# First 512 tokens from four batches instead of four chunks of one: a recurrence with a feed-forward layer on one core

## The chip, the cores and the metric

The kernel runs on one core of a Trainium2 chip. The time is device microseconds (us), the median of several executions. The kernel before took 190.63 us (three runs, 190.18 to 190.70) when the prediction was made and 190.66 beside the changed kernel (four runs, one of them in the slow state with 193.85). The ratios below use runs in the fast state alone.

## The reference

Gated linear attention (four batches, eight heads, 768 tokens, head size 48), then a feed-forward layer with a squared relu on the 3072 tokens.

```python
for t in range(S):                                   # q, k, v, alpha: [4, 8, 768, 48]
    state = alpha[:, :, t, :, None] * state + np.einsum('bhd,bhe->bhde', k[:, :, t], v[:, :, t])
    y[:, :, t] = np.einsum('bhd,bhde->bhe', q[:, :, t], state)
x = y.transpose(0, 2, 1, 3).reshape(3072, 384)
out = np.maximum(x @ w_in, 0.0) ** 2 @ w_out         # w_in 384 x 2048, w_out 2048 x 384
```

## The kernel before

Tokens are worked on in 24 chunks of 128. For a chunk, ScalarE takes the logarithm of alpha, TensorE sums it up along the tokens, ScalarE makes the exponentials A and 1/A, VectorE multiplies q and k with them, TensorE transposes both and forms scores, VectorE masks these, and TensorE multiplies with v and reads and updates the state. The result is transposed (xT) and goes through the feed-forward layer. A scheduler in the kernel, which works with fixed durations, fixes the order of instructions on each engine. What it costs when the next one in that order has to wait is seen below (ScalarE lost 13.7 us so).

The first four chunks are done together, with wide first loads, and are the four chunks of one batch, so their state updates follow one another:

```python
slot_srcs = {n: a[0, :, 0:4 * P, :].rearrange("h (p j) d -> p h (j d)", j=4) for n, a in srcs}
...
def load_slots(nm, lo, hi):                  # two of these for alpha and two for q
    nc.sync.dma_start(out=slot[nm][:, lo:hi].rearrange("p h j d -> p h (j d)"),
                      in_=slot_srcs[nm][:, lo:hi])
```

Later chunks have four loads each. SyncE issues alpha, q and k as fp32 (five buffers each); GpSimd issues v, which its queue casts to bf16 on the way (six buffers). SyncE also issues the output, one write per tile of 128 rows:

```python
LB = 5; LBV = 6
...
(nc.gpsimd if pool or nm == "vt" else nc.sync).dma_start(out=d[nm], in_=src[b, c])
...
nc.sync.dma_start(out=out_r[GT[g] + tt], in_=box["ob"])
...
hold_x(C[6], C[5], "at")      # SyncE's loads of chunk 6 and later start when chunk 5's alpha is there
```

## Time and profile before

| | before |
|---|---|
| time, span | 190.63 us, 189.4 us |
| TensorE, VectorE, ScalarE, GpSimd busy | 95%, 70%, 67%, 22% of the span |
| first feed-forward matmul | 22.50 us |
| TensorE in every stretch from 60 us to 172 us | full |

The prediction below shows the busy tenths, the chain and the start. What it does not show, and what turned out to matter, is the loads of later chunks. These are lines of the timeline of SyncE (start, us of issuing, queue, line, transfer): the alpha loads of chunks 10 to 13.

```profile
54.70 0.59 SPq L339 DMA_DIRECT2D at<-in_alpha_dram  x1
...
57.38 1.63 SPq L339 DMA_DIRECT2D at<-in_alpha_dram  x1
...
62.40 1.70 SPq L339 DMA_DIRECT2D at<-in_alpha_dram  x1
...
66.56 1.07 SPq L339 DMA_DIRECT2D at<-in_alpha_dram  x1
```

Alpha is a chunk's first load and first need. Here one follows the other about every 4 us, and in the stretch from 20 to 100 us ScalarE's logarithm is never listed as waiting for one. TensorE in two stretches (length, then busy time and count of PE, PEld, DVE, ACT, POOL, then TensorE's clock, DMA share, GB/s):

```profile
60.00:74.00 14.00, 14.00 (x168) 10.94 (x166) 11.59 (x26) 10.71 (x27) 3.73 (x6) 1.00 1.34 173
74.00:88.00 14.00, 14.00 (x159) 10.73 (x157) 11.70 (x31) 10.25 (x32) 3.90 (x8) 1.00 1.30 187
```

### The profile page before, as it was taken

The page shows a single profiled execution, that of the slowest core. Times are in us where ns is not written, and L with a number is a line of the kernel's source. Part 1 is how long each engine was busy: PE and PEld are TensorE (multiplying, and loading weights), DVE is VectorE, ACT ScalarE, POOL GpSimd, SP SyncE. Part 2 cuts the span into 40 slices and gives each one's busy share as a digit, 9 for nine tenths or more (in the row PEclk, how much of TensorE's full clock was granted, in tenths as well). Part 3 has the DMA queues.
Part 4 walks back from the last instruction along what each step waited for, and adds up shares of the span by engine and source line. Part 5 has one row for each costly group of instructions (what it writes and reads, how often), then busy time and mean ns, then how long its engine had stood idle before and what let it go on. Part 6 is the DMA issues. An engine that isn't in the chain of part 4 may idle for free.

```text
span 189.4 us, 5215 instructions
## 1 busy us (share of the span) xinstructions
PE 180.2 (95%) x1999; PEld 137.1 (72%) x1999; DVE 132.3 (70%) x335; ACT 126.7 (67%) x346; POOL 42.2 (22%) x78
## 2 busy tenths in 40 slices
PE   7864999999999999999999999999999999999993
PEld 2553778866878887777777787787787787777773
DVE  3167946754899795897886886886886886944411
ACT  3763459926778886678588588488588586565630
POOL 8967335023122233222021031041000000000000
PEclk9998589999999999999999999999999999999999
DMA  5999999899999999999959739739011011011112
GB/s 177 238 165 203 204 223 211 125 183 147 183 191 185 206 180 173 201 153 188 218 130 142 166 84 124 170 87 126 0 45 43 3 42 45 6 37 45 42 42 83
DMA packets 94280, 24.71 MB, mean 130 GB/s; under 512 B 85216, under 2 KB 93920, under 8 KB 94256
## 3 DMA queue, kind: packets, MB, share of 16 engines
q1 hardware_dynamic: 64992, 17.45, 44.8%
q0 software_dynamic: 29120, 6.88, 37.5%
q8 instruction: 15, 0.25, 0.6%
q14 instruction: 9, 0.07, 0.1%
q10 hardware_dynamic: 144, 0.05, 0.1%
HBM read 25.17 MB, written 4.72 MB: 158 GB/s over the span
## 4 chain that ended last, share of the span: by engine, by line
PE 87%; DMA 5%; SPq 3%; ACT 1%; DVE 1%; issue 1%; ACTq 0%; DVEq 0%
PE bank L226 78%; PE bank L229 7%; DMA kt<-in_k_dram 5%; PE st L226 2%; SPq L339 2%; SPq L319 1%; ACT r L668 1%; DVE st L578 1%; DVE sm L533 1%; ACT sb L583 0%; ACT xn L220 0%; DVE ob L736 0%; ACT ob L736 0%; ACT L_s L442 0%; DVE kI_s L474 0%
## 5 line engine op out<-in xcount | busy, mean ns | idle before, releaser
L668 ACT ACTIVATE r<-bank 128x256 bf16<-128x256 f32 (+1 forms) x160 | 64.7, 429 | 29.6 <-PE bank L226 28.2
L226 PE MATMUL bank<-xT_big,w_in_b 128*128 128x256 bf16 (+1 forms) x624 | 80.0, 266 | 0.1
L226 PE MATMUL bank<-w_out_b,gT 128*128 128x384 bf16 (+1 forms) x400 | 74.7, 320 | 0.0
L226 PEld LDWEIGHTS <-w_in_b 128*128 128x128 bf16 x624 | 53.8, 98 | 9.7 <-issue 0.5
L675 DVE TENSOR_TENSOR gT<-r 128x256 bf16<-128x256 bf16 (+1 forms) x160 | 47.6, 315 | 16.0 <-ACT r L668 14.4
L226 PEld LDWEIGHTS <-gT 128*128 128x128 bf16 x400 | 37.9, 98 | 15.8
L533 DVE TENSOR_TENSOR sm<-bank,utri_b 128x512 bf16<-128x512 f32 x40 | 25.3, 683 | 2.6 <-PE bank L226 2.5
L339 POOL DMA_DIRECT2D vt<-in_v_dram x24 | 21.3, 888 | 7.9 <-POOL vt L338 6.1
L338 POOL CAST vt<-kt 128x1 bf16<-128x1 f32 x18 | 4.7, 263 | 64.6 <-PE bank L226 41.8
L471 DVE TENSOR_TENSOR qA_s<-qt,A 128x384 bf16<-128x384 f32 x20 | 11.1, 556 | 9.5 <-ACT A L458 8.6
L218 DVE COPY qkT<-bank 128x1024 bf16<-128x1024 bf16 x20 | 13.8, 688 | 4.9 <-PE bank L229 4.9
L474 DVE TENSOR_TENSOR kI_s<-kt,Ainv 128x384 bf16<-128x384 f32 x24 | 13.3, 556 | 3.1 <-DMA kt<-in_k_dram 2.6
L709 ACT COPY ob<-bank 128x384 f32<-128x384 f32 x21 | 10.1, 480 | 8.1 <-PE bank L226 8.1
L226 PEld LDWEIGHTS <-qkT 64*128 64x128 bf16 (+1 forms) x260 | 10.4, 97 | 5.9 <-issue 2.5
L220 ACT CAST xn<-bank 128x384 bf16<-128x384 f32 x23 | 10.9, 480 | 4.2 <-PE bank L226 3.8
L583 ACT CAST sb<-st 128x384 bf16<-128x384 f32 x20 | 9.6, 478 | 5.7 <-DVE st L578 5.7
L458 ACT ACTIVATE A<-bank 128x384 bf16<-128x384 f32 x20 | 9.9, 496 | 2.4 <-PE bank L226 2.4
L229 PE MATMUL bank<-ident_bf,kI_s 128*128 128x128 bf16 x96 | 9.5, 223 | 2.1 <-DVE kI_s L474 2.1
L578 DVE TENSOR_TENSOR st<-st,ae_s 128x384 f32<-128x384 f32 x20 | 11.1, 556 | 0.0
L442 ACT ACTIVATE L_s<-at 128x384 bf16<-128x384 f32 x20 | 10.4, 521 | 0.0
L462 ACT ACTIVATE Ainv<-bank 128x384 bf16<-128x384 f32 x20 | 10.2, 510 | 0.0
L229 PE MATMUL bank<-ident_bf,qA_s 128*128 128x128 bf16 x96 | 9.3, 219 | 0.8 <-DVE qA_s L407 0.7
(78 smaller groups left out, 162.1 us busy)
## 6 DMA issues: line engine op xcount, KB each, us to landing
out_dram<-ob SPq DMA_DIRECT2D x23, 192.0 KB, 2.7
kt<-in_k_dram SPq DMA_DIRECT2D x21, 192.0 KB, 5.3
at<-in_alpha_dram SPq DMA_DIRECT2D x18, 192.0 KB, 4.8
qt<-in_q_dram SPq DMA_DIRECT2D x18, 192.0 KB, 4.7
vt<-in_v_dram POOLq DMA_DIRECT2D x24, 96.0 KB, 5.6
w_in_b<-in_moe_w_in_dram POOLq DMA_DIRECT2D x4, 384.0 KB, 11.0
w_out_b<-in_moe_w_out_dram POOLq DMA_DIRECT2D x4, 384.0 KB, 12.3
slot_at<-in_alpha_dram SPq DMA_DIRECT2D x2, 384.0 KB, 3.6
```

The costliest lines, as they stand in the source:

```text
L218: pin(nc.vector.tensor_copy(out, in_))
L220: pin(nc.scalar.copy(out, in_))
L226: pin(nc.tensor.matmul(*a, **kw))
L229: pin(nc.tensor.transpose(*a))
L339: pin((nc.gpsimd if pool or nm == "vt" else nc.sync).dma_start(out=d[nm], in_=src[b, c]))
L442: pin(nc.scalar.activation(L[:, :, 0:D], d["at"], AF.Ln))
L471: pin(nc.vector.tensor_mul(qA[:, :, 0:D], d["qt"], d["A"]))
L474: pin((nc.vector if mk.eng == "DVE" else nc.gpsimd).tensor_mul(kI[:, :, 0:D], d["kt"], d["Ai"]))
L533: pin(nc.vector.tensor_mul(d["sm"][:, hh], d["sc"][hh], (utri_p if first else utri_b).to_broadcast([P, NP, P])))
L578: pin(nc.vector.tensor_mul(st4, st4, bcast(ae, D)))
L668: pin(nc.scalar.activation(box["r"], box["ph"], AF.Relu))
L675: pin(nc.vector.tensor_mul(gT[g][:, f0:f0 + nf, 0:n], box["r"], box["r"]))
```

## The change

The intent is to rid the start of the chain of four state updates: the first chunk of each batch needs no state, so the four first chunks can be done side by side. Partition 4g+b holds the four consecutive tokens 4g to 4g+3 of batch b. Several things come with it: each of alpha, q and k is loaded by four DMAs over 32 partitions, v comes as fp32, through SyncE's queue for all chunks but 4 and 5 (GpSimd loads these two), and is cast by GpSimd (for two of the first four chunks by ScalarE), there are four load buffers instead of five (and four for v instead of six), and the output of the first four tiles, whose rows are out of order, is written in four pieces each.

```diff
-    slot_srcs = {n: a[0, :, 0:4 * P, :].rearrange("h (p j) d -> p h (j d)", j=4) for n, a in srcs}
+    rows = {n: a[:, :, 0:P, :].rearrange("b h (g j) d -> b g h (j d)", j=NJ) for n, a in srcs}
+    v_rows = v[:, :, 0:P, :].rearrange("b h (g j) d -> j g (b h) d", j=NJ)
+    SEQ = [(b, 0) for b in range(B)] + [(b, c) for b in range(B) for c in range(1, NCH)]
-    LB = 5
-    LBV = 6
+    LB = 4
-    opool = ctx.enter_context(tc.tile_pool(name="opool", bufs=8))
+    opool = ctx.enter_context(tc.tile_pool(name="opool", bufs=5))
...
+            pin(q.dma_start(out=slot[nm][b::B], in_=rows[nm][b]))          # b = 0..3; 32 partitions each
...
-                pin((nc.gpsimd if pool or nm == "vt" else nc.sync).dma_start(out=d[nm], in_=src[b, c]))
+                pin((nc.gpsimd if pool else nc.sync).dma_start(out=C[s][nm], in_=srcs[nm][c, :, b * H:(b + 1) * H]))
...
+        def e_vb():
+            d["vb"] = work.tile([P, H, D], BF16, name="vb", bufs=4)
+            pin(nc.gpsimd.tensor_copy(d["vb"], d["vt"]))
...
-            pin(nc.sync.dma_start(out=out_r[GT[g] + tt], in_=box["ob"]))
+            if SEQ[GT[g] + tt][1] == 0:
+                for j in range(NJ):
+                    pin(nc.sync.dma_start(out=out_tile(GT[g] + tt)[j], in_=ob[j * PQ:(j + 1) * PQ]))
+            else:
+                pin(nc.sync.dma_start(out=out_tile(GT[g] + tt), in_=ob))
```

## The prediction

> **What bounds the kernel now.** I read the page's busy tenths first, then the chain that ended last in order of time, then the first 30 us of the timeline.
>
> ```profile
> PE   7864999999999999999999999999999999999993
> DVE  3167946754899795897886886886886886944411
> PEclk9998589999999999999999999999999999999999
> DMA  5999999899999999999959739739011011011112
> ```
>
> Each digit is 4.73 us. TensorE is full from the fifth slice on; only the first four have holes, and slice 5 runs at half clock. The DMA engines are busy for half the run, but TensorE does not wait for them after the start. The chain says where the start ends:
>
> ```profile
> 6.33 9.01 DMA kt<-in_k_dram
> 15.50 0.34 issue
> 15.84 0.56 DVE st L578
> 16.40 0.96 DVE sm L533 x2
> ...
> 22.50 15.27 PE bank L226 x139
> ...
> 167.36 18.95 PE bank L226 x152
> 186.33 0.25 ACT ob L736
> ```
>
> Until 22.50 the path is a load (the third k tile, 9.01 us from issue to landing), then the state chain of four sequential chunks; from 22.50, the first feed-forward matmul, it is TensorE to 186.3. A table of stretches confirms it (us, busy and counts of PE, PEld, DVE, ACT, POOL, then clock, DMA, GB/s):
>
> ```profile
> 16.00:22.50 6.50, 5.49 (x63) 3.88 (x63) 6.23 (x12) 3.81 (x9) 3.08 (x5) 0.64 1.25 206
> 22.50:40.00 17.50, 17.50 (x168) 13.99 (x169) 11.20 (x25) 12.13 (x25) 6.28 (x9) 0.94 1.18 187
> ```
>
> So the time is: start (22.5) + TensorE work left at that moment + tail (3.0, to 189.4), and the device time is 1.2 above the span (190.63 against 189.4). After 22.5 come 163.8 us. Steady state has a period of 13.94 us for two tiles (the same piece of the chain, 4.83 us of feed-forward matmuls, begins at 100.28 and again at 114.22), 6.97 per tile, of which streaming 48x128 plus 16x384 columns at the full rate is about 5.2 and attention about 1.75. 24x5.2 + 20x1.75 + 2.8 left from the first four chunks = 162.6, plus 1.1 for half clock until 24.7: 163.7. The sum closes, so nothing else is hidden there. The change can gain only (a) by an earlier start, (b) by less TensorE work after it.
>
> **What the Trainium skill says.** "TensorE: Matmul & The Clock Gate", Part 1, has the clock halved after an idle window and restored after about 3.4 us of sustained activity. The trace agrees: granted clock 0.53 in the stretch 20 to 25 us, 1.00 from 25 on. The same must be paid again after any new start. "DMA: Bandwidth & Descriptors", section Issuing engines are not separate DMA queues, says that loads from several issuers share the same 16 engines and only issue time is saved; here the k tile that took 9.01 us was issued by SyncE while GpSimd had v and k tiles under way, which fits. "SBUF — State Buffer", section Who interferes with whom, says that a VectorE instruction with two SBUF inputs contends with a GpSimd instruction that reads SBUF. No trace of before shows it (GpSimd's only casts are 128x1); the change makes it possible. The same page, section Door 1: The DMA port swizzle, charges strided reads that leave a 16-byte line. The trace fits: the three matmuls that transpose xn against a strided identity take 0.81 us even at full clock, 390 ns each against 219 for a plain transpose.
>
> **The change part by part.**
>
> Removed: the four chunks of one batch as the first 512 tokens, with their state chain (4 rounds of matmul, 0.56 VectorE, 0.48 ScalarE) between 15.8 and 22.3 us. In its place stand the first chunks of four batches, which need no state. Their state updates, and the transposes back of k that they need, move behind the start of the feed-forward part.
>
> TensorE work, from durations back to back at full clock (transpose 0.056, state matmul 0.043, score 0.04, 48-column 0.032, 96-column 0.06, 384-column 0.16, 4-column 0.03 us). Before, first four chunks: 16 matmuls of 32 rows, about 0.6; 16 cumulative of 384 columns, 2.6; 32 transposes 1.8; 16 sums 0.5; scores 1.3; sm x v 1.0; state reads 0.7; state 0.7; the strided xn transposes 12x0.27 = 3.2: 12.4. After: the 32-row ones are gone; cumulative 2.7 in 28 pieces; transposes 1.8; sums 0.5; scores 1.3; sm x v 1.0; plain xn transposes 12x0.056 = 0.7: 8.0. Later 16 transposes of k 0.9, state 0.7, state reads 0.7: 10.3 in all. Work saved 2.1, but it is saved in the start. Left over once the feed-forward part runs (read off the timeline after 22.5): before 2.8, of which two strided xn transposes are 1.6; after 2.3 plus the end of chunks three and four, 0.6: 2.9. Part (b) is nil. **The gain is the start alone.**
>
> Start after, step by step. Alpha: before, its halves (393 KB each) landed at 4.13 and 5.30, so 336 GB/s; now four pieces, two of them behind ScalarE's 1.28 us table load: about 5.2. ScalarE is then the busiest engine: 4 logs at a pitch of 0.43 (7.0), 8 exponentials at 0.42 and two small ones at 0.2 (10.8), six copies at 0.48 (13.7). K lands after 2x786 KB more at 336 GB/s, 4.7 us: 9.9; VectorE then makes four k products and the last q product at a pitch of 0.5 (12.4), its transpose 0.4, its copy is ScalarE's last, done about 13.8. Scores 0.4 (14.2); the masks' second halves, 4x0.36 on VectorE (15.8); product with v 0.4 twice (16.6); xn 0.5, transpose 0.4, xT 0.5 and a few hand-overs: **first feed-forward matmul at 18.2** (17.2 to 20). Before: 22.5. Gain 4.3.
>
> The weights are now held until k has landed: issued from 10 us, so w_in's first quarter (before: issued 8.85, landed 8.7 later behind v and k tiles) should land at 15 to 17 with only v in its way. Just in time. v is 786 KB in 192-byte pieces, about 4 us after k: 14; its casts are then not the last thing.
>
> Against that: half clock. VectorE and ScalarE pace TensorE from 10 to 18 us, so it will be cold again; before, 2.2 us at half clock fell after 22.5 (loss 1.1). Starting at 18.2, I expect about 4 us cold: loss 2.0, so 0.9 more. And 0.7 for new holes (below). Sum: -4.3 + 0.9 + 0.7 = -2.7; 190.6 - 2.7 = **187.9 us**.
>
> Beside other work: v is loaded as fp32 by SyncE (24.7 MB become about 27, but no casting queue), and 22 casts of 128x384 go to GpSimd, which is 22% busy. From a 128x128 select at 0.30 and a 128x512 iota at 0.57 I estimate 0.5 each, 11 us in all, off the path. Output rows in four pieces for the first four tiles: issue time on SyncE, off the path.
>
> **The rivals.**
>
> *A late weight takes the place of the wait.* If k lands at 12 rather than 10 (small pieces on 32 partitions being slower than 336 GB/s), everything after shifts by 2, and w_in, held behind it, lands at 18 to 19 or later. The start would be 20.5 to 22 and the time 189.5 to 191. For it: k is the end of before's path. Against it: 768-byte pieces instead of 192, and no GpSimd traffic beside them.
>
> *VectorE becomes the bound.* In program order it gets 15 output copies instead of 2 (13x0.56 = 7.3 us more, ScalarE 6.3 less) and meets the casts' reads. In the fullest stretch it was busy 17.36 of 20 us; 13 copies over 110 us add about 1.3 per 20. 93% plus lock waits could open holes in TensorE: 1 to 4 us, 189 to 191.5. Against it: its waits were mostly for ScalarE's relu, which gets lighter. I charge 0.7 of it, with late chunk 4 and 5 loads and the run of first-layer matmuls on which ScalarE's relu leaves little slack.
>
> *The start is better than worked out.* If TensorE stays warm and ScalarE's two alpha loads issue at once, the start is 17 and no cold loss: 185.5 to 186.5.
>
> **Range and chances.** The centre is 187.9 (1.4% less); the 2% line is at 186.8, 1.1 below it. The start's uncertainty is 1.2, the clock's 1, the holes' 1; together about 1.8. Range 185.9 to 190.2. Faster by over 2%: 0.28; within: 0.62; slower by over 2% (194.4, only if VectorE or the loads starve TensorE for over 6 us): 0.10.
>
> **What would show it.** First feed-forward matmul near 18 us; clock 0.5 for some 4 us about it; the chain before it through ScalarE and VectorE, with no state line; TensorE without holes afterwards; xn transposes near 220 ns; casts near 0.5 us. I am wrong if that first matmul waits for w_in, if TensorE shows waits for VectorE in 60 to 160, or if the start is at 18 and the time still the same.

## The result, and the profile after

The changed kernel took 199.02 us (median of four runs, 197.50 to 200.06) against 190.66: slower, ratio 1.044 with a 95% interval of 1.035 to 1.053. Ratios here are the mean time of one kernel's fast runs over the mean of the other's fast runs of the same rounds, so they are not quite the ratio of the medians. The result is correct. The profiled run took 197.5 us with a span of 195.8. It is the fastest of the four: the other spans are 196.2 to 198.2, and no trace shows where these runs lost more.

The busy tenths of the changed kernel (a digit is 4.9 us):

```profile
PE   7776999999997947999999999999999999999993
DVE  5199479686975916797788798897897888855531
PEclk9996699999999996999999999999999999999999
DMA  5999999989997979999589379659610011011112
```

TensorE now has a hole where the line of before had only nines: slices 13 to 16 read 7, 9, 4, 7, at 59 to 78 us. VectorE dips there too, to 5 and 1, so it is not VectorE's load that holds TensorE up. The rest of the line is full. The stretches of before, again:

```profile
60.00:74.00 14.00, 9.59 (x105) 7.33 (x103) 8.22 (x21) 9.02 (x21) 1.19 (x2) 1.00 0.86 160
74.00:88.00 14.00, 13.38 (x125) 10.14 (x126) 10.88 (x26) 7.95 (x25) 1.01 (x2) 0.88 1.29 204
```

TensorE is busy for 9.59 of 14 us, then loses more to a clock of 0.88 and another 0.6 us of idling. The chain that ended last, asked for this stretch alone (start, us, what):

```profile
55.69 0.42 SPq L772
...
56.21 4.09 DMA at<-in_alpha_dram
...
60.38 0.52 ACT L_s L500
60.91 0.97 ACT r L718 x2
...
65.22 0.43 SPq L772
...
66.78 5.63 DMA at<-in_alpha_dram
...
72.86 0.58 ACT r L718
```

The path leaves TensorE. It goes through SyncE's queue issuing output pieces (L772), then an alpha load of 4 to 5.6 us, then ScalarE's logarithm of it (L500), then the relu of the feed-forward layer (L718), which stands behind that logarithm in ScalarE's order. The longest hole shows the same from both sides, in the timelines of ScalarE and TensorE:

```profile
72.43 0.52 ACT L500 ACTIVATE L_s<-at 128x384 bf16<-128x384 f32 x1 [4.11 <-DMA at<-in_alpha_dram]
...
74.62 0.50 PE L210 MATMUL bank<-ident_bf,xn 128*128 128x128 bf16 x3 [3.75 <-ACT xn L201]
```

ScalarE waits 4.11 us for the alpha of chunk 12, and TensorE 3.75 us for the copy xn, which also stands behind that logarithm (it runs at 74.07). In the list of waits for 20 to 100 us there is a line that before has not (total us, count, longest):

```profile
ACT L_s L500 <- DMA at<-in_alpha_dram: 13.7, 7, 4.1
```

SyncE's timeline tells why alpha is late:

```profile
53.88 2.23 SPq L772 DMA_DIRECT2D out_dram<-ob  x4
56.21 0.40 SPq L431 DMA_DIRECT2D at<-in_alpha_dram  x1
56.65 0.58 SPq L431 DMA_DIRECT2D qt<-in_q_dram  x1
57.33 3.21 SPq L772 DMA_DIRECT2D out_dram<-ob  x4
60.59 0.42 SPq L431 DMA_DIRECT2D kt<-in_k_dram  x1
61.11 0.53 SPq L431 DMA_DIRECT2D vt<-in_v_dram  x1
61.73 0.75 SPq L431 DMA_DIRECT2D at<-in_alpha_dram  x1
...
66.78 0.92 SPq L431 DMA_DIRECT2D at<-in_alpha_dram  x1
...
73.69 0.65 SPq L431 DMA_DIRECT2D at<-in_alpha_dram  x1
```

SyncE issues almost without a gap. Alpha of chunks 10 to 13 goes out at 56.2, 61.7, 66.8 and 73.7, where before it went out at 54.7, 57.4, 62.4 and 66.6: some 5.8 us apart instead of 4. The four groups of four pieces (two are shown; the others took 2.30 and 3.59 us) hold SyncE for 11.3 us in all between 53.9 and 72.2, and the v loads for another part. The pieces were not late themselves: their tiles had been copied out by 49.7, 52.0, 55.9 and 60.2, and their first pieces went out at 53.9, 57.3, 63.3 and 68.6.

The start, from the timelines of ScalarE, VectorE and TensorE:

```profile
6.72 1.76 ACT L341 ACTIVATE L_f<-slot_at 128x384 bf16<-128x384 f32 x4 [4.64 <-DMA slot_at<-in_alpha_dram]
...
11.75 1.96 DVE L361 TENSOR_TENSOR qk_f<-slot_kt,Ainv 128x384 bf16<-128x384 f32 x4 [0.48 <-ACT ae L395]
...
16.91 0.92 ACT L201 CAST vb<-v 128x384 bf16<-128x384 f32 x2 [1.46 <-DMA v<-in_v_dram]
...
20.44 0.80 PE L207 MATMUL bank<-xT_big,w_in_b 128*128 128x256 bf16 x3 [0.25 <-ACT xT_big L201]
```

Alpha is there at 6.7, k at about 11.7, v at 16.9, and the first feed-forward matmul runs at 20.44, 2.06 us earlier than before.

**Where the time went.** I added up, for each trace, what TensorE's matmuls cost at full rate (columns over 2400 us plus 2.5 ns, at least 32 ns: 0.163 us for 384 columns, 0.109 for 256 and 0.056 for 128, which are the distances between the starts of such matmuls back to back in both traces; for 48 columns the traces have 0.025, so the small ones are charged too much; warm-up matmuls count nothing). It is an estimate, made the same way for all kernels. The sum is the work; the time minus the work done so far is what TensorE has lost by then.

| | work in all | lost by 30 us | by 60 | by 81 | at the end |
|---|---|---|---|---|---|
| before | 175.4 | 13.6 | 13.7 | 13.4 | 14.0 |
| after | 173.7 | 14.0 | 14.7 | 21.4 | 22.1 |

The work fell by 1.7 us, the loss by 30 us rose by 0.4: the new start is worth 1.3 us. Between 30 and 81 us the changed kernel loses 7.4 us and the other gains 0.2 (the cost at full rate is slightly overestimated), so the new holes cost 7.6. The sum is 6.3, and the spans differ by 6.4.

### The profile page after: what moved, and what is told of

It is laid out like the page before. It is cut to its first block, busy times and chain, and to the rows that moved or that the text cites. A ratio compares the mean times of both kernels' runs of the same rounds, so it can differ in the third digit from the quotient of the medians.

```text
span 195.8 us, 5297 instructions
## 1 busy us (share of the span) xinstructions
PE 181.7 (93%) x2011; PEld 138.9 (71%) x2011; DVE 143.2 (73%) x357; ACT 124.4 (64%) x340; POOL 30.4 (16%) x56
## 4 chain that ended last, share of the span: by engine, by line
PE 68%; DMA 18%; SPq 5%; ACT 3%; issue 2%; POOL 2%; DVE 1%; POOLq 0%; ACTq 0%
PE bank L207 61%; DMA at<-in_alpha_dram 11%; PE bank L210 6%; DMA w_in_b<-in_moe_w_in_dram 5%; SPq L319 3%; DMA slot_kt<-in_k_dram 2%; SPq L772 2%; PE st L207 2%; ACT r L718 1%; POOL w_in_b L269 1%; ACT L_s L500 1%; SPq L431 1%; DVE kI_s L527 0%; ACT A L511 0%; ACT Ainv L515 0%
## 5 line engine op out<-in xcount | busy, mean ns | idle before, releaser
L718 ACT ACTIVATE r<-bank 128x256 bf16<-128x256 f32 (+1 forms) x160 | 64.6, 429 | 28.3 <-PE bank L207 27.2
L207 PE MATMUL bank<-w_out_b,gT 128*128 128x384 bf16 (+1 forms) x400 | 75.7, 322 | 0.0
L725 DVE TENSOR_TENSOR gT<-r 128x256 bf16<-128x256 bf16 (+1 forms) x160 | 49.2, 329 | 19.3 <-ACT r L718 17.5
L493 POOL CAST vb<-vt 128x384 bf16<-128x384 f32 x20 | 12.2, 609 | 99.9 <-PE bank L207 65.3
L500 ACT ACTIVATE L_s<-at 128x384 bf16<-128x384 f32 x20 | 10.4, 521 | 13.7 <-DMA at<-in_alpha_dram 13.7
L199 DVE COPY qkT<-bank 128x1024 bf16<-128x1024 bf16 x20 | 13.7, 686 | 3.5 <-PE bank L210 3.4
L524 DVE TENSOR_TENSOR qA_s<-qt,A 128x384 bf16<-128x384 f32 x20 | 11.4, 569 | 3.4 <-ACT A L511 2.7
L762 DVE COPY ob<-bank 128x384 f32<-128x384 f32 x15 | 8.4, 557 | 7.5 <-PE bank L207 7.4
L210 PE MATMUL bank<-ident_bf,xn 128*128 128x128 bf16 x72 | 8.4, 234 | 4.2 <-ACT xn L201 4.2
L527 DVE TENSOR_TENSOR kI_s<-kt,Ainv 128x384 bf16<-128x384 f32 x20 | 12.0, 598 | 0.3
L199 DVE COPY xT_big<-bank 128x384 bf16<-128x384 bf16 x22 | 7.6, 351 | 3.7 <-PE bank L210 3.5
L210 PEld LDWEIGHTS <-xn 128*128 128x128 bf16 x72 | 5.5, 103 | 6.7 <-ACT xn L201 5.3
L207 PE MATMUL bank<-vb,sm 128*128 128x48 bf16 x192 | 9.3, 189 | 0.1
```

The source lines that it names most:

```text
L199: pin(nc.vector.tensor_copy(out, in_))
L207: pin(nc.tensor.matmul(*a, **kw))
L210: pin(nc.tensor.transpose(*a))
L493: pin(nc.gpsimd.tensor_copy(d["vb"], d["vt"]))
L500: pin(nc.scalar.activation(L[:, :, 0:D], d["at"], AF.Ln))
L524: pin(nc.vector.tensor_mul(qA[:, :, 0:D], d["qt"], d["A"]))
```

## The experiments

Three theories of the holes stood at first. A: the output pieces delay the loads behind them in SyncE's queue. B: v as a fourth load in that queue does. C: four load buffers let the loads run less far ahead. The first four runs took one part away from the changed kernel, or put one into the other. All of them were run with their own runs of the kernel before on the same chip, whose medians were 190.7, 191.54, 191.41 and 190.69 us in the four batches of runs.

### The pieces away: one write per tile, rows in the wrong places

```diff
-            if SEQ[GT[g] + tt][1] == 0:
-                for j in range(NJ):
-                    pin(nc.sync.dma_start(out=out_tile(GT[g] + tt)[j], in_=ob[j * PQ:(j + 1) * PQ]))
-            else:
-                pin(nc.sync.dma_start(out=out_tile(GT[g] + tt), in_=ob))
+            b, c = SEQ[GT[g] + tt]
+            pin(nc.sync.dma_start(out=out_r[b * NCH + c], in_=ob))
```

> The changed kernel with the first four output tiles written by one DMA each instead of four pieces; the rows land in the wrong order, so the result is wrong on purpose. Theory A (the sixteen pieces in SyncE's queue hold the alpha loads behind them up): the holes of TensorE between 60 and 88 us (5.0 us idle and 1.7 us of half clock) go nearly away, 190 to 192.5 us. Theory B (a fourth load per chunk, v, in SyncE's queue) and theory C (four load buffers instead of five): holes stay, 196 us or more.

Measured: wrong result, as meant; 194.12 us, ratio 1.020 (1.016 to 1.024). Neither A nor B nor C as stated: 4.9 of the 8.3 us of the loss went. TensorE was busy for 11.95 us of the stretch from 60 to 74, and ScalarE still waited 8.3 us for alpha.

### The pieces away, correctly: rows put in order when xT is copied

```diff
-            copy(d["x"], xT_big[:, :, s * P:(s + 1) * P], d["px"])
+            xs, px = xT_big[:, :, s * P:(s + 1) * P], d["px"]
+            if first:
+                copy(d["x"], xs.rearrange("p k (g j) -> p k j g", j=NJ), px.rearrange("p k (j g) -> p k j g", j=NJ))
+            else:
+                copy(d["x"], xs, px)
```

and one write per tile as above.

> The rows are put back in order where xT is copied out of PSUM for the first four tiles, so one DMA each writes them, and the result is right. Theory A: within 1 us of e1_one_write_wrong_rows, 190 to 193 us; the four strided copies of xT cost below 0.3 us each. Theories B and C: 196 us or more.

Measured: correct, 194.02 us, ratio 1.020 (1.016 to 1.024). The holes are gone altogether here, but the start has become later:

```profile
20.59 1.86 ACT L201 COPY xT_big<-bank 128x384 bf16<-128x384 bf16 x2 [0.21 <-PE bank L210]
```

Two copies with 8-byte steps in the output take 1.86 us where two plain ones took 0.86 us in the changed kernel. The first feed-forward matmul comes at 22.51 and the clock stays half until about 28 us. The loss is 17.5 by 30 us and 17.6 by 81. So a start that is 2.7 us later than in the run before it gave the loads the time that they lacked, and the total is the same. Alpha of chunk 13 was issued at the same time in both runs, 68.2 and 68.0. That is a first sign that the loads set 194 in both, wherever the waiting falls.

### v away from SyncE's queue

```diff
+    LBV = 6
...
-                pin((nc.gpsimd if pool else nc.sync).dma_start(...))
+                pin((nc.gpsimd if pool or nm == "vt" else nc.sync).dma_start(...))     # vt a bf16 tile, cast by the queue
...
-            vb = d["use_vt"] = add("POOL", 0.52, e_vb, d["ld_vt"], ...)
+            vb = d["ld_vt"]                                                            # no cast on GpSimd
```

> The changed kernel, pieces kept, with v of chunks 4 to 23 loaded as before by a casting DMA of GpSimd, so that SyncE's queue has three loads per chunk. Theory A: at most a third of the loss comes back, 195 to 199 us. Theory B: 188 to 192 us, no hole at 60 to 88 us. Theory C: no change, 197 to 200 us.

Measured: correct, 194.03 us, ratio 1.020 (1.014 to 1.025), TensorE busy for 11.77 us from 60 to 74. Again about half, though the pieces are still there.

### The pieces put into the kernel before

```diff
-            pin(nc.sync.dma_start(out=out_r[GT[g] + tt], in_=box["ob"]))
+            for j in range(NJ if GT[g] + tt < NJ else 1):
+                w = PQ if GT[g] + tt < NJ else P
+                pin(nc.sync.dma_start(out=out_r[GT[g] + tt][j * w:(j + 1) * w], in_=box["ob"][j * w:(j + 1) * w]))
```

> The kernel before with its first four output tiles written in four pieces of 32 rows each (result right). Theory A: alpha loads land later and TensorE gets holes, 193 to 198 us. Theories B and C: 190 to 191.5 us.

Measured: correct, 191.41 us, ratio 1.003 (1.000 to 1.006), TensorE full in both stretches. The pieces do cost queue time here as well:

```profile
50.41 2.23 SPq L716 DMA_DIRECT2D out_dram<-ob  x4
52.74 1.52 SPq L339 DMA_DIRECT2D at<-in_alpha_dram  x1
```

but SyncE has three loads per chunk here, not four, and alpha of chunk 13 still goes out at 68.76. The kernel before also bears lateness better: in its fixed order on ScalarE, the logarithm of chunk 10 stands behind 26 relus and that of chunk 13 behind 34, in the changed kernel behind 22 and 32 (counted in the two traces). No run tested that this is why. A alone fell with this run. The new theory, D: the pieces and v in SyncE's queue together make the loads late; each is worth about 4.5 to 5 us in the changed kernel, and without both the holes are gone.

### The pieces issued by GpSimd

```diff
-                    pin(nc.sync.dma_start(out=out_tile(GT[g] + tt)[j], in_=ob[j * PQ:(j + 1) * PQ]))
+                    pin(nc.gpsimd.dma_start(out=out_tile(GT[g] + tt)[j], in_=ob[j * PQ:(j + 1) * PQ]))
```

> The changed kernel with the sixteen pieces issued by GpSimd instead of SyncE; v stays with SyncE. After the first four runs I hold theory D: what counts is SyncE's queue of loads, of which each DMA waits for the one eight before it; pieces and v loads both cost places in it, and TensorE is starved because the loads of chunks 10 to 12 come late. Theory D: like e1_one_write_wrong_rows, 193 to 195 us, with some 2 us of holes left at 60 to 88 us. Theory A' (it is the writes themselves, 1536 bytes from 32 partitions, not the queue's places): 196 us or more.

Measured: correct, 193.45 us, ratio 1.014 (1.010 to 1.018). The same pieces with the same bytes do from another queue no more harm than taking them away leaves. So it is not the writes' traffic in the DMA engines that hurts, but their place in SyncE's queue. The DMA engines were not at their limit either: from 60 to 74 us they moved 160 GB/s in the changed kernel, 204 here and 200 with the pieces away.

### Less lead

```diff
-    LEAD = 4
+    LEAD = 3
```

> The changed kernel, one number changed: a chunk may be up to three tiles ahead of the feed-forward part instead of four, so the same loads are asked for later by about one tile (7 us); loads and pieces as they are. Theory D: the holes at 60 to 88 us shrink to under 2 us, 191 to 195 us. Theory A' (pieces hold the DMA engines, whoever waits): 197 us or more.

Measured: correct, 209.63 us, ratio 1.097 (1.093 to 1.101). The expectation was wrong. A row of the table of stretches:

```profile
116.00:130.00 14.00, 12.76 (x146) 9.77 (x145) 11.78 (x31) 9.43 (x28) 1.49 (x2) 1.00 0.65 140
```

TensorE has holes past 170 us, long after the loads are done. With less lead a chunk's own chain of engines seems no longer hidden, whatever the loads do. The run says nothing on D.

### Rows in order by a permuted identity

```diff
+    by_token = consts.tile([P, P], BF16)       # the identity with its columns permuted, made once by GpSimd
...
+                if first:
+                    mm(d["px"][:, j, :], lhsT=d["xn"][:, j * P:(j + 1) * P], rhs=by_token, start=True, stop=True)
+                    continue
```

and one write per tile. The permuted identity is the moving operand here.

> The changed kernel with rows put back in order by a contiguous permuted identity as the moving operand of the xn transposes of the first four tiles (a plain matmul into fp32), one write per tile, result right. Theory D: as e1_one_write_wrong_rows, 193.5 to 195 us, without e2_rows_in_order's late start (1.06 us for each strided copy of xT on ScalarE against 0.48).

Measured: correct, 194.14 us, ratio 1.017 (1.014 to 1.021), like the version with wrong rows. It keeps the copies plain and costs nothing that shows in the time, though its first feed-forward matmul came at 21.17 against 19.79.

### Both away: rows by the identity, and v by GpSimd's queue

The two edits above together.

> e12_rows_by_identity and e4_v_by_casting_dma together: neither pieces nor v loads in SyncE's queue. Theory D: the effects add, no hole over 0.5 us at 60 to 88 us, 189 to 191.5 us, as good as before. If the loss were something else that the two only happen to touch (chunk order, four buffers, GpSimd's casts): 193 us or more.

Measured: correct, 191.52 us (15 runs), ratio 1.002 (0.999 to 1.004).

```profile
60.00:74.00 14.00, 14.00 (x162) 11.23 (x160) 12.35 (x30) 10.97 (x28) 3.75 (x8) 1.00 1.33 191
74.00:88.00 14.00, 14.00 (x161) 10.53 (x160) 10.72 (x29) 9.35 (x27) 3.39 (x7) 1.00 1.24 184
```

TensorE is full again, with the same order of matmuls as in the changed kernel. D stands: the two together are the holes. (Taking v away also took GpSimd's casts of it away and gave v six buffers; no run parted these. But no wait of TensorE in the changed kernel from 20 to 190 us is put down to GpSimd.) Side by side (the first column of numbers is the time; then the alpha load of chunk 13, and ScalarE's waits for alpha from 20 to 100 us):

| | time, us | alpha of chunk 13 issued | waits for alpha |
|---|---|---|---|
| changed kernel | 199.0 | 73.7 | 13.7 |
| v away | 194.0 | 69.3 | 5.3 |
| pieces by GpSimd | 193.5 | 68.2 | 8.4 |
| pieces away, rows wrong | 194.1 | 68.0 | 8.3 |
| both away | 191.5 | 65.9 | 1.9 |

Without the holes the changed kernel is as fast as the kernel before, no faster: the new start, for which the change was made, gives nothing there. Its first feed-forward matmul comes at 21.52, only 0.98 us earlier than before, and state work that used to precede that matmul now follows it (see the part on the prediction). The next runs looked at that, and at what was left of C.

### Five load buffers

```diff
-    LB = 4
+    LB = 5             # v stays at four, output buffers four instead of five
```

> Correct result: the changed kernel with five load buffers for alpha, q and k (as in the kernel before) instead of four, v kept at four, the output buffers four instead of five to make room. Theory C (four buffers let the loads run less far ahead, so they come late): the holes between 60 and 81 us go, 191 to 194. Theory D (the narrow stores and the v loads in SyncE's queue delay the loads by the places in flight and issue time, whatever the buffers): TensorE still about 9 to 11 of 14 us busy in 60:74 and the time 197 to 200.

Measured: correct, 198.10 us, ratio 1.034 (1.029 to 1.040), TensorE busy for 10.21 us from 60 to 74. C fell, D's figure held.

### SyncE's loads released earlier

```diff
-                hold_x(C[6], C[5])
+                hold_x(C[6], C[4])
```

> Correct result: the changed kernel with SyncE's stream of loads (chunk 6 on) released by the arrival of chunk 4's alpha instead of chunk 5's, so some 8 us earlier. Theory D (the stream is late by the time the narrow stores and v take in it): a head start makes up for it, TensorE over 12 of 14 us busy in 60:74, time 192 to 197; the earlier loads can take bandwidth from chunk 5's loads and the last weights, so the hole between 30 and 40 us may grow by up to 2 us. If the holes are made by something local to 60 to 81 us (DMA engines too slow there, evictions), a head start changes nothing: 198 to 200.

Measured: correct, 199.68 us, ratio 1.044 (1.041 to 1.048). D's figure was missed, but the head start was not obtained either:

```profile
28.57 0.40 SPq L431 DMA_DIRECT2D at<-in_alpha_dram  x1
...
33.19 8.33 SPq L431 DMA_DIRECT2D vt<-in_v_dram  x1
41.55 1.25 SPq L431 DMA_DIRECT2D at<-in_alpha_dram  x1
```

SyncE begins at 28.6 instead of 36.3, but its fourth load, v of chunk 6, takes 8.33 us to issue, and the second chunk's alpha goes out at 41.55, against 41.35 in the changed kernel. Until then the DMA engines were busy with weights and chunk 5 (206 GB/s from 30 to 40 us). What held that one instruction the trace does not say; the DMA issued eight before it, whose landing it has to await, had landed at 12.0. The run does not tell D from its rivals.

### The start: wide first loads

Predicted was a start at 18.2 us from arrival times (alpha 5.2, k 9.9) that came from the rate of the wide alpha loads before. So the version with both away was run with wide loads, which fetch other tokens of the same size.

```diff
-            pin(q.dma_start(out=slot[nm][b::B], in_=rows[nm][b]))            # four per tensor
+            hs = slice(b * H // 2, (b + 1) * H // 2)
+            pin(q.dma_start(out=slot[nm][:, hs], in_=wide[nm][:, hs]))       # two per tensor, 128 partitions
```

> Wrong result on purpose: the version whose holes are gone (rows in order by a stationary permuted identity, v by the casting queue), with alpha, q and k of the first 512 rows fetched as the kernel before fetches them, each in two loads over all 128 partitions (other tokens, same bytes), instead of four loads over 32 partitions each. It tests the size that my prediction gave the start: it took the arrival times of wide loads (alpha at 5.2, k at 9.9 us) for the narrow ones. If the narrow loads are what made the start late: alpha by 5.0 to 5.8 (7.0 in the version with narrow loads), k by 9.5 to 10.5 (12.5), the first feed-forward matmul 1.5 to 2.5 us earlier than its 21.52, thus 19 to 20, and the time 189.5 to 191.0. If the start is late for another reason (the masks on GpSimd and VectorE, the length of the chain behind k), alpha and k land earlier but the first matmul stays above 20.7 and the time within 0.5 us of 191.5.

(In what ran, the permuted identity is the moving operand, not the stationary one; and the kernel before loaded only alpha and q wide, k came chunk by chunk.)

Measured: wrong result, as meant; 199.50 us, ratio 1.044 (1.038 to 1.050): neither expectation. Alpha came at 4.06 and 5.24 as expected, but the weights, which are held until k has landed, looked at the first half of k only. They were issued from 10.6 us on, beside v, and v landed at 25.7. My edit had put a new wait into the start. It is a lesson in itself, but no test.

### The start: two queues for the narrow q loads

```diff
-    ld_qt = [load_batch("qt", b, nc.sync, 1.7) for b in range(B)]
+    ld_qt = [load_batch("qt", b, nc.sync if b % 2 == 0 else nc.scalar, 1.7) for b in range(B)]
```

> Correct result: the version whose holes are gone, with two of the four narrow q loads issued by ScalarE, which has nothing to do until alpha lands, so that SyncE issues k about 1.3 us earlier. Nothing else moves; every other engine has the same order. If issue time on SyncE is what delays k: k lands at 11.0 to 11.6 instead of 12.5, first feed-forward matmul at 20.3 to 21.0 instead of 21.5, and the time 190.5 to 191.3 (0.3 to 1 us better than with all q loads on SyncE). If the narrow loads are slow in the DMA engines themselves, k lands at about 12.5 still and the time is unchanged.

Measured: correct, 191.97 us, ratio 1.004 (1.001 to 1.006). K landed at 13.06, not at 11.0 to 11.6, and alpha came later, at 8.16 instead of 7.0. SyncE began with k 0.9 us earlier, at 3.94, but its four k loads took 4.73 us to issue instead of 2.65: each of the k loads waits for the landing of an alpha load, because the DMAs issued by SyncE and ScalarE take eight semaphores in turn and each waits for the one eight before it, and alpha was now later. So the last alpha landed at 8.05 by the trace's semaphore events and the last k load went out at 8.07, instead of 6.91. Room on SyncE alone brings nothing here; the run can't say what k would do if it were truly issued earlier.

### The start: wide loads with the weights held properly

Three runs: wide loads with the weights held until v has landed, narrow loads with the same hold, and wide loads with the weights held until all of k has landed.

```diff
-        pin(nc.gpsimd.tensor_copy(w_in_b[:, 0, 0:1], slot["kt"][:, 0, 0:1]))
+        pin(nc.gpsimd.tensor_copy(w_in_b[:, 0, 0:1], v_0[:, B - 1, H - 1, 0:1]))      # first two runs
+        pin(nc.gpsimd.tensor_copy(w_in_b[:, 0, 0:1], slot["kt"][:, H - 1, 0:1]))      # third run
```

> Wrong result on purpose: wide first loads as before, but the weights are held until v has landed. To be read against the run with narrow loads and the same hold. If the narrow loads make the start late: alpha by 5.3, all of k by 11.0, v by 14.5 (16.9 to 17.4 where the loads were narrow), the first feed-forward matmul at 18.0 to 19.5 and 1.2 to 2.5 us earlier than with narrow loads, the time lower by about as much (189 to 191). If v's small pieces or the chain behind k set it whatever the loads: the first matmul within 0.7 us of the narrow version.

> Correct result: the version whose holes are gone, with narrow first loads, weights held until v has landed instead of k. Control for the wide one. V at 15.5 to 17, the first weights issued right behind it and landing 2.5 to 3 us later, so the first feed-forward matmul at 20.5 to 22 and the time 191 to 193; if w_in takes the place of v as the last arrival, the first matmul waits for w_in by the profile.

> Wrong result on purpose: wide first loads, weights held until the second half of k has landed (the earlier run looked at the first half). If the early weights were what starved v there: v lands by 17 to 18.5 instead of 25.7, the first feed-forward matmul at 19 to 21 and the time 190 to 192. If v in 192-byte pieces is starved by any weight load behind it: v at 20 or later, time 193 to 198.

Measured: 196.93 us (wrong as meant, one of its four runs in the slow state, ratio 1.030, 1.022 to 1.038), 196.77 us (correct, 1.030, 1.022 to 1.037) and 193.48 us (wrong as meant, 1.014, 1.007 to 1.021).

| | alpha | last of k | v | first two xT copied from | first feed-forward matmul |
|---|---|---|---|---|---|
| wide, weights after v | 5.2 | 11.4 | 16.6 | 19.1 | 22.84, waits for w_in |
| narrow, weights after v | 6.8 | 13.0 | 16.9 | 20.7 | 23.10, waits for w_in |
| wide, weights after k | 5.2 | 12.9 | 17.0 | 20.1 | 21.00 |
| narrow, weights after k (both away) | 7.0 | 12.5 | 17.4 | 20.6 | 21.52 |

Wide loads bring alpha 1.6 to 1.8 us earlier. K doesn't follow reliably: rows one and three do not differ in anything before k has landed, and yet it came at 11.4 and 12.9, so its scatter is as large as the effect. V comes between 16.6 and 17.4 in all four. Where k is early too (first row), xT is ready 1.6 us before that of the narrow version, and then the weights bind; in the last two rows the wide loads gain 0.5 us at the first matmul. That is within the scatter of single traces: the changed kernel and five runs that leave its start alone (wrong rows, v away, pieces by GpSimd, five buffers, less lead) have that matmul between 19.79 and 20.74. So the narrow loads are at most a small part of the late start. Alpha and k, v, and the weights all come within 2 us of the point at which they would set the start, and taking one away shows the next. (The third run's time is nevertheless 2 us longer than that of the narrow version: TensorE ends 0.4 us later, 186.7 against 186.3, and its last write, issued at 187.3, takes until 191.4, 1.7 us more than the other's. I have no explanation for that write.)

The larger part seems to be how long the transfers take; no run changed the piece size of v to test it. The table of stretches for the second run, in which no weights run beside v:

```profile
8.00:10.00 2.00, 2.00 (x12) 1.35 (x11) 0.56 (x1) 1.59 (x5) 0.00 (x0) 0.50 1.06 323
...
14.00:16.00 2.00, 1.81 (x24) 1.13 (x24) 2.00 (x5) 1.99 (x4) 0.00 (x0) 1.00 0.75 108
```

Alpha, q and k, in pieces of 768 bytes, move at 314 to 323 GB/s (6 to 10 us); v, in pieces of 192 bytes, at 139 and then 108 (12 to 16 us; the last of them landed at 16.9). The Trainium skill's page "DMA: Bandwidth & Descriptors", section Specifications, names 512 bytes as the least for full rate. The trace agrees. The times of the two kernels with the weights after v, 197, come mostly from what the later weights delay in turn (by the sum above, 3.6 and 5.1 us lost between 30 and 81 us).

No version beat the kernel before. The version with both parts away is level with it, with an interval from 0.999 to 1.004.

## Why the prediction was wrong

Predicted was 187.9 us with a range up to 190.2; the changed kernel took 199.0.

**What bounds the kernel: right for the kernel before.** There TensorE was full from the start on. In the changed kernel "start plus TensorE work plus tail" leaves 7.6 us over, the holes, which the prediction had at 0.7.

**"Part (b) is nil", work saved 2.1: nearly right.** The work fell by 1.7 us by the estimate above (which charges the strided xn transposes of before like plain ones; their starts lie about 0.21 us apart in the trace, the prediction had 0.27). What was left after the first feed-forward matmul was by the same estimate, with 0.16 us more for each of the six strided transposes that fell there, 165.3 us before and 165.9 after: 0.6 more, where the prediction had 0.1.

**The start at 18.2, gain 4.3: mechanism right, size wrong.** The state chain is gone from the start, but the first matmul came at 20.44. The term that was mis-sized is the arrival of data. "Alpha: about 5.2" measured 6.7, "K lands at 9.9" measured 11.7, and "v is 786 KB in 192-byte pieces, about 4 us after k: 14; its casts are then not the last thing" measured 16.9, with its casts done at 17.4 to 17.9, as late as the masks and scores, which end at 17.4 to 18.0. From k to the first matmul 8.3 us were predicted and 8.7 passed, so the steps behind k came out right in sum; with v as late as the masks, that is partly luck. My rate of 336 GB/s came from two wide loads and was carried over to narrow ones, and the 4 us for v amount to 197 GB/s (786 KB) where 192-byte pieces reached 108 to 139. The rival "a late weight takes the place of the wait" had k at 12 and the start at 20.5 to 22, and both came nearly so. Its other half did not come: the first matmul waited 0.25 us for ScalarE's xT copy, not for w_in. Its reason for k, small pieces on 32 partitions, is not shown: with wide loads k came at 11.4 and at 12.9.

**Half clock, 0.9 more: wrong.** The clock records of the traces have half clock from 16.02 to 22.85 us in the changed kernel and from 17.88 to 24.70 before: 6.83 us in both. What counts in the prediction's sum is the part after the first feed-forward matmul. It was to grow from 2.2 to about 4 us and was 2.41, so it cost 0.1 us more, not 0.9. The 0.9 too much hid part of what the start lacked. Start and clock together were to give 3.4 us; the new start gave 1.3 by the table: 2.06 from the earlier matmul, less 0.6 of work and 0.1 of clock.

**"0.7 for new holes", and "off the path" for two things: this is the step that failed.** The prediction says of the output "Output rows in four pieces for the first four tiles: issue time on SyncE, off the path", and of v "loaded as fp32 by SyncE ... no casting queue ... off the path". Both went into the queue that also issues alpha, q and k, in order, and together they made alpha 1.5, 4.4, 4.4 and 7.1 us late. Alpha's logarithm stands in ScalarE's order ahead of the relu and the xn copy that TensorE needs. The holes and the clock lost in them cost 7.6 us instead of 0.7. The run with both parts away shows it; the two with one part away show that each leaves about half. The prediction did name the case, "only if VectorE or the loads starve TensorE for over 6 us", with a chance of 0.10, but not what would bring it about. Late loads were named in the sum only for chunks 4 and 5; the loss from 30 to 40 us, about 1 us, is there, but the rest came at chunks 10 to 13.

**VectorE becomes the bound: did not happen.** It makes 15 of the output copies (8.4 us) as foreseen, but from 20 to 190 us TensorE's waits for VectorE come to 0.7 us in all, and in the steady stretches it is busy for 12 of 14 us with TensorE full. Transposes of xn took 234 ns (220 predicted), casts 609 ns (500).

What a piece costs the queue is its issue time, as far as the trace tells, and not its place among the transfers in flight. Each of SyncE's DMAs waits for the landing of the one issued eight before it, but by the semaphore events in the trace of the changed kernel every DMA that SyncE issued from 50 to 80 us came at least 1.05 us after that landing. Eleven of the sixteen pieces took 0.41 to 0.43 us to issue, five took 0.84 to 1.81. What stays open is why those five took longer, and which part of the v edit counts (its loads in the queue, its casts or its buffers).

## What to carry to other kernels

When a change adds transfers to a queue that also issues loads, count that queue in order, instruction by instruction, as one counts an engine: here a store of a quarter of the bytes took 0.41 us or more to issue, a whole one in the kernel before 0.36 or more, and the load behind it is what pays. When one cause explains half of a loss and another cause explains half too, run them out together before looking for a third. And take the rate of a transfer from one with the same piece size: here 192-byte pieces moved at 108 to 139 GB/s and 768-byte ones at 314 to 323.

## What the Trainium skill lacked or had wrong

- "DMA: Bandwidth & Descriptors", section Issuing engines are not separate DMA queues, says that issuing from several engines saves only the time to initiate a DMA, usually small. Here moving 16 narrow stores from SyncE to GpSimd took the time from 199.0 to 193.5 us, because the loads behind them in program order came earlier by up to 5.5 us. The section says nothing of what a store costs the loads that its issuer has behind it.
- The same page gives no time for issuing by shape. Here SyncE took 0.42 to 0.51 us for a first load over 128 partitions (393 KB each) and 0.60 to 0.72 for one over 32 partitions with half of the bytes; the shortest later loads took 0.37 us, and one took 8.33.
- The same page's section Specifications says that pieces under 512 bytes fall below full rate, without a measured rate for them. Here 192-byte pieces ran at 108 to 139 GB/s and 768-byte ones at 314 to 323.
- "SBUF — State Buffer", section Who interferes with whom, has VectorE instructions with two SBUF inputs contend with GpSimd's reads, without saying how much to expect in a mixed kernel. With 12.2 us of GpSimd casts of v, the product of k and 1/A took 598 ns on average, against 556 before and 556 again in the run with v away, which has no such casts for the later chunks.
- "TensorE: Matmul & The Clock Gate", Part 1, gives about 3.4 us of sustained activity for the way back to full clock. In both starts half clock lasted 6.83 us, twice as long: TensorE was busy for 5.2 of the 6 us from 16 to 22 in the changed start and stayed at half clock until 22.85. Nor was it idle when the clock fell: it was busy for 2.20 of the 3.42 us before that. How much work the page's windows count as activity it does not say, and no run tested it.
- "SBUF — State Buffer", section Door 1: The DMA port swizzle, has accesses of bf16 data stride for free up to eight elements. Here two xT copies on ScalarE that write bf16 in steps of four elements (8 bytes) took 1.86 us, two plain ones 0.86, so it did not hold for these writes.
